# Filler matmuls and a re-weighted planner in a fused attention, MLP and convolution kernel

## The chip, the cores and the metric

One core of a Trainium2 chip runs the kernel. The metric is the device time of one execution in microseconds, median of three runs.

## The reference

Three stages follow one another, for 4 batches of 768 tokens and a model width of 384 (8 heads of 48):

```python
f = 1.0 / (1.0 + np.exp(-f_logit))                       # gated linear attention
for t in range(S):
    state = f[:, :, t, :, None] * state + np.einsum('bhd,bhe->bhde', k[:, :, t], v[:, :, t])
    y[:, :, t] = np.einsum('bhd,bhde->bhe', q[:, :, t], state)
...
xn = (x - mu) / np.sqrt(var + 1e-06) * g_ln              # layer norm, MLP of width 1536
x = x + np.maximum(xn @ w_ch1, 0.0) @ w_ch2
...
h = np.maximum(x @ w_in, 0.0)                            # width 1024
conv_out[s] = sum of conv_w[k] * h[s + k - 1], k = 0, 1, 2
out = (h * (1 / (1 + np.exp(-conv_out)))) @ w_out
```

The weights arrive as float64 and are decoded on the chip.

## The kernel before

The 3072 tokens are cut into 24 chunks of 128 (six to a batch), and three chunks make a unit, eight in all. `chunk(t)` (L467) computes the attention of one chunk: ScalarE (ACT) forms the gates, VectorE (DVE) runs two scans over them (L499, L501), GpSimd (POOL) or VectorE multiplies queries and keys by the products (L505, L507), two more VectorE operations finish the keys (L509, L511), and TensorE (PE) computes the scores (L525), the products of keys and values (L557 or L598 to L600) and the outputs (L626, L636 or L655). GpSimd computes the reciprocal deviation of the layer norm (L673, L677), and a transposing DMA brings the normalized chunk to the MLP.

`first(u)` is the first matrix of the MLP (L716 to L718, three half-precision products for one accurate one), `second(u, tt)` the second (L785 to L791), `gate(u)` the input matrix of the convolution (L845 to L847), the taps on VectorE (L862, L867), the gate, and the output matrix (L896 to L898). `prep1` and `prep` decode the weights in 22 pieces: a DMA brings a piece (L391), three VectorE operations decode it (L397, L400, L403), ScalarE and VectorE split it in a high and a low half, and for the first matrix TensorE forms the low half with diagonal matrices (L430, L431) that `diags` makes on ScalarE (L920). The conv table (L927 to L931) is one more small piece. The gates can't start before the last piece is decoded, since their buffers lie in the memory of the decoding.

No instruction order is written by hand. Every step is a `Job` with an engine, a guessed duration, a key, what it depends on and the buffers it takes. `Plan.run` (L172) simulates the engines with the guessed durations, and at every step issues the job that could start first; among jobs of one engine that could start within 0.1 us of the first, the one with the lowest key. The order so found is the program of each engine, and the hardware runs it with semaphores. The keys are due times in microseconds: `CP` and `CPL` are the pace of the chunks (`CPL` from the twelfth), `C1` and `C2` set the two MLP matrices of later units back, `H2` the gates, `O` the output matrix, `EV` brings evictions forward, `W1`, `W2` and `WI` are the due times of the weight pieces, whose loads have a key 30 lower. A job on POOL also sets the simulated VectorE back by a share of its duration. The six PSUM banks of pool `B` go to whatever asks first.

Of the kernel before, what the change touches and what calls it, by code (L numbers as in the profile page):

```python
# [9 lines left out]
F32 = mybir.dt.float32  # L10
F16 = mybir.dt.float16
BF16 = mybir.dt.bfloat16
# [7 lines left out]
B, H, S, D = 4, 8, 768, 48  # L20
DM = H * D
# [38 lines left out]
XN_ACT = range(0, 10)  # L60
X2_PE = range(0, 9)
OBX = 2
SW = CH + 1


CP = 22.6
CPL = 22.0
LATE = 12.0
T0 = 32.5
ATT = 0.3  # L70
C1 = 63.0
C2 = 19.7
H2 = -23.6
O = 46.1
EV = 38.7
W1 = 23.8
W2 = 52.3
WI = 95.7

def flat(a):  # L80
    return a.rearrange("p a b -> p (a b)")
# [2 lines left out]
def decode(nc, dst, tmp, raw):  # L84
    hi = raw[:, :, 1]
    nc.vector.tensor_scalar(
        out=tmp, in0=hi, scalar1=3, scalar2=0x3FFFFFFF,
        op0=ALU.logical_shift_left, op1=ALU.bitwise_and,
    )
    nc.vector.scalar_tensor_tensor(  # L90
        out=tmp, in0=hi, scalar=-0x40000000, in1=tmp, op0=ALU.bitwise_and, op1=ALU.bitwise_or
    )
    nc.vector.scalar_tensor_tensor(
        out=dst.bitcast(U32), in0=raw.bitcast(U32)[:, :, 0], scalar=29, in1=tmp.bitcast(U32),
        op0=ALU.logical_shift_right, op1=ALU.bitwise_or,
    )
# [19 lines left out]
class Job:  # L116
    def __init__(self, eng, dur, key, fn, deps, takes, uses, lat):
        self.eng, self.dur, self.key, self.fn, self.lat = eng, dur, key, fn, lat
        self.takes, self.uses = takes, uses
        self.left, self.then, self.ready, self.at = 0, [], 0.0, None  # L120
        for d in deps:
            d.then.append(self)
            self.left += 1


class Plan:
# [9 lines left out]
    def __init__(self):  # L136
        self.pools = {}
        self.n = 0
        self.jobs = []

    def slots(self, name, tiles):
# [20 lines left out]

    def start(self, j, free):
        t = max(j.ready, free)
        for p, k in j.takes:
            s = self.pools[p]
            if not s.free or (p not in self.ANY and s.order[0] != k):
                return None
            t = max(t, s.free[0][0])
        return t  # L170

    def run(self):  # L172
        ready = {e: [] for e in self.ENGINES}
        free = dict.fromkeys(self.ENGINES, 0.0)
        for j in self.jobs:
            if not j.left:
                ready[j.eng].append(j)
        todo = len(self.jobs)
        while todo:
            best = None  # L180
            for e in self.ENGINES:
                c = [(t, j.key, z) for z, j in enumerate(ready[e])
                     if (t := self.start(j, free[e])) is not None]
                if not c:
                    continue
                first = min(c)[0]
                pick = min((k, t, z) for t, k, z in c if t <= first + 0.1)
                if best is None or pick[1] < best[0]:
                    best = (pick[1], e, pick[2])
            assert best  # L190
            t, e, z = best
            j = ready[e].pop(z)
            for p, k in j.takes:
                s = self.pools[p]
                s.order.remove(k)
                s.held[k] = s.free.pop(0)[1]
            j.fn()
            j.at = t
            free[e] = t + j.dur
            if e == "POOL":  # L200
                free["DVE"] += 0.2 * max(0.0, j.dur - 0.8)
            end = t + j.dur + j.lat
            for p, k in (*j.takes, *j.uses):
                s = self.pools[p]
                s.users[k] -= 1
                s.last[k] = max(s.last.get(k, 0.0), end)
                if not s.users[k]:
                    s.free.append((s.last[k], s.held[k]))
                    s.free.sort()
            for x in j.then:  # L210
                x.left -= 1
                x.ready = max(x.ready, end)
                if not x.left:
                    ready[x.eng].append(x)
            todo -= 1
        return max(free.values())
# [3 lines left out]
def fast_path(  # L220
    ctx: ExitStack, tc: tile.TileContext, v, qk_, f_, gln, w1, w2, wi, cw, wo, out, bad
):
    nc = tc.nc
    const = ctx.enter_context(tc.tile_pool(name="const", bufs=1))
# [3 lines left out]
    P = Plan()  # L228
# [6 lines left out]
    V = lambda n: 0.07 + n * 1.04e-3  # L235
    V2 = lambda n: 0.07 + n * 0.53e-3
    A = lambda n: 0.1 + n * 0.833e-3
    G = lambda n: 0.15 + n * 2.2e-3

    fbs = bufs("fb", 2, [128, NP, SW], F32)  # L240
    qks = bufs("qk", 2, [128, 2, NP, CH], F32)
    nc.vector.memset(fbs[0][:, :, 0:1], 20.0)
    nc.vector.memset(qks[0], 0.0)
    mhalf = const.tile([128, 1], F32, name="mhalf")
    warm = const.tile([128, 1], F32, name="warm")
    nc.gpsimd.memset(mhalf, -0.5)
# [25 lines left out]
    gl8 = const.tile([128, KC], F32, name="gl8")  # L272
    cws = const.tile([128, M2, 3], F32, name="cws")
# [5 lines left out]
    pall = const.tile([128, NT, NP, 1], F32, name="pall")  # L279
# [37 lines left out]
    diag = pp.tile([128, KC, 128], F32, name="diag")  # L317
# [32 lines left out]
    J = {}  # L350
# [20 lines left out]
    def check_raw(g):  # L371
        nc.scalar.activation(  # L372
            out=g, in_=g, func=AF.Square, scale=RAW_MAX ** -0.5, accum_out=acc_col()
        )
        nc.scalar.activation(
            out=g, in_=g, func=AF.Exp, scale=-RAW_MAX / RAW_MIN, accum_out=acc_col()
        )

    def transfer(dur, key, fn, buf, size):
        j = P.job("SP", dur, key, fn, (), [buf], lat=1.0)  # L380
        return P.job("DMA", size / 2.8e5, key, lambda: None, [j], (), [buf], lat=1.2)

    def words(name, a, src, key):
# [83 lines left out]
    def chunk(t):  # L467
        b, c = divmod(t, NCH)
# [3 lines left out]
        key = due_att(t)  # L472
        N = NP * CH
        fb = lambda: flat(P("fb", t))
        e = lambda: flat(P("e", t))
# [5 lines left out]
        pend = lambda: P("e", t)[:, :, CH:]  # L481
# [6 lines left out]
        def tt(n, dk, fn, deps, takes=(), uses=(), pool=True):  # L488

            if pool:  # L490
# [8 lines left out]
        s1 = P.job("DVE", 1.14, key + 4, lambda: nc.vector.tensor_tensor_scan(  # L499
            e(), e(), flat(d1), 1.0, ALU.mult, ALU.max), [a2], (), [E_])  # L500
        s2 = P.job("DVE", 1.14, key + 5, lambda: nc.vector.tensor_tensor_scan(  # L501
            w(), w(), flat(d2), 1.0, ALU.mult, ALU.min), [a4], (), [W_])
        P.job("POOL", 0.8, key + 30, lambda: nc.gpsimd.tensor_copy(pall[:, t], pend()), [s1], (),
              [E_])
        qe = tt(N, 6, lambda v_: v_.tensor_tensor(out=q_(), in0=q_(), in1=e3(), op=ALU.mult),  # L505
                [s1, J["qk", t]], (), [E_, Q_], t in POOL_Q)
# [38 lines left out]
        if not last and not dma:  # L545
# [23 lines left out]
            else:  # L569
                j = dv(DM, 14, lambda: nc.vector.scalar_tensor_tensor(  # L570
                    out=tm()[:112], in0=kv3(), scalar=SY, in1=so()[:112], op0=ALU.mult,
                    op1=ALU.add), [kv, *old], (), [K_, KV, *SO])
# [88 lines left out]
        x = lambda: P("x", t)  # L661
# [3 lines left out]
        ST, RS = ("st", t), ("rs", t)  # L665
# [10 lines left out]
            )  # L676
            nc.gpsimd.tensor_tensor(out=rs, in0=rs, in1=mhalf, op=ALU.pow)  # L677
        bn = P.job("DVE", 0.69, key + 19, stats, [xc], [ST], [X_])
        rs = P.job("POOL", 1.0, key + 20, rstd, [bn], [RS], [ST])
        N_, XS = ("xn", t), ("xs", t)  # L680
        if t in XN_ACT:
            MB = ("mb", t)
            mb = P.job("POOL", 0.41, key + 20, lambda: nc.gpsimd.tensor_scalar(
                out=P(*MB), in0=mv[:, 0:1], scalar1=P(*RS), scalar2=-1.0, op0=ALU.mult,
                op1=ALU.mult), [rs], [MB], [RS])
            scaled = lambda o, dk, deps, takes, uses: act(
                DM, key + dk, o, x, AF.Identity, deps, takes, [*uses, X_, RS, MB],
                scale=lambda: P(*RS), bias=lambda: P(*MB))
            xn = scaled(lambda: P(*N_), 21, [mb], [N_], [])
            xh = scaled(lambda: P(*XS)[:, 0], 22, [mb], [XS], [])  # L690
            xh = P.job(None, 0.0, key + 22, lambda: None, [xn, xh])
        else:
            xn = dv(DM, 21, lambda: nc.vector.tensor_scalar(
                out=P(*N_), in0=x(), scalar1=mv[:, 0:1], scalar2=P(*RS), op0=ALU.subtract,
                op1=ALU.mult), [rs], [N_], [X_, RS], lambda n: 0.39)
            xh = act(DM, key + 22, lambda: P(*XS)[:, 0], lambda: P(*N_), AF.Copy, [xn], [XS], [N_])
# [218 lines left out]
    craw = const.tile([128, M2 * 3, 2], I32, name="craw")  # L915
# [4 lines left out]
    def diags():  # L920
# [2 lines left out]
                out=diag[:, kc, :], in_=ident, func=AF.Copy, scale=gl8[:, kc:kc + 1]  # L923
            )
        nc.scalar.activation(out=nident, in_=ident, func=AF.Copy, scale=-1.0)
    J["diag"] = P.job("ACT", 1.2, -10.0, diags, [J["gl8"]])
    cj = P.job("SP", 0.45, 20.0, lambda: nc.sync.dma_start(  # L927
        out=craw.rearrange("p n t -> p (n t)"), in_=cw.bitcast(I32)))
    cj = P.job("DVE", 0.5, 60.0, lambda: decode(nc, cws.rearrange("p a b -> p (a b)"), ctw, craw), [cj])

    P.job("ACT", 0.9, 70.0, lambda: check_raw(craw.bitcast(F32)[:, :, 1]), [cj])  # L931

    for m in range(6):
        J["w1", m] = prep1(m, W1 + 4.0 * m)
# [39 lines left out]
    for i, w_ in enumerate((w1s, w2s, wis, wos)):  # L974
        h_ = w_[:, 0].rearrange("p a b -> p (a b)")
        n = h_.shape[1] // 6
        for z in range(6):
            norm2(lambda h_=h_, z=z, n=n: h_[:, z * n:(z + 1) * n], n, 1.0, nrm[:, i, z:z + 1],
                  500.0 + z, [J["late"]])
    with tc.manual_schedule():  # L980
        P.run()

# [269 lines left out]
```

## Time and profile before

| | us |
|---|---|
| runs | 624.65, 625.05, 627.04 |
| median | 625.05 |
| profiled execution | 625.46 |
| its span | 623.8 |
| TensorE busy | 586.1 (94%) |
| VectorE busy | 495.9 (80%) |
| ScalarE busy | 395.7 (63%) |
| GpSimd busy | 95.4 (15%) |

The span runs from the first to the last instruction; the profiled execution's own time is 1.66 us longer. Busy shares are means over a front, in which VectorE is nearly always busy and TensorE has gaps, and a long later stretch in which TensorE has none. In the groups below, a time in square brackets at the end of a timeline row is how long the engine sat idle before it, and after the arrow stands what ended that.

### The profile page before, as it was taken

How to read it: one execution, taken by the hardware profiler on the slowest of the kernel's cores; microseconds unless marked ns; L12 is line 12 of the kernel's file. 1: busy time of each engine (PE TensorE's matmuls, PEld its weight loads, DVE VectorE, ACT ScalarE, POOL GpSimd, SP SyncE). 2: the span in 40 equal slices, each digit the busy share in tenths (PEclk: the TensorE clock that was granted, in tenths of full speed). 3: DMA queues.
4: the chain of work that ended last, by engine and by line, in shares of the span. 5: the costliest groups of instructions: out<-in, count | busy, mean ns of one | idle time of the engine just before them, and what ended most of it. 6: DMA issues, size and time to landing. Idle time of an engine off the chain costs nothing.

```text
span 623.8 us, 11788 instructions
## 1 busy us (share of the span) xinstructions
PE 586.1 (94%) x4698; PEld 398.0 (64%) x4698; DVE 495.9 (80%) x753; ACT 395.7 (63%) x808; POOL 95.4 (15%) x142
## 2 busy tenths in 40 slices
PE   0889999899899999999999999999999999999994
PEld 0769777677576666666666666666666666666562
DVE  4797999999998998599899995698996942315962
ACT  3697877789899975364596863554684722315762
POOL 4451342423343100100000100010000000000000
PEclk9998999899999999999999999999999999999999
DMA  8573746870234023453422106432311002002011
GB/s 222 162 184 119 230 147 168 232 193 14 56 84 115 22 59 100 102 104 89 94 56 68 56 14 124 110 78 59 68 40 56 14 1 64 25 1 40 1 38 44
DMA packets 77951, 53.83 MB, mean 86 GB/s; under 512 B 51520, under 2 KB 69952, under 8 KB 77888
## 3 DMA queue, kind: packets, MB, share of 16 engines
q1 hardware_dynamic: 77888, 53.00, 34.2%
q8 instruction: 39, 0.64, 0.4%
q14 instruction: 24, 0.20, 0.1%
HBM read 36.20 MB, written 4.72 MB: 66 GB/s over the span
## 4 chain that ended last, share of the span: by engine, by line
PE 69%; DVE 21%; ACT 3%; DMA 2%; issue 2%; POOL 1%; SPq 0%; POOLq 0%
PE B L716 6%; PE B L717 6%; PE B L718 6%; PE B L788 6%; PE B L790 6%; PE B L791 6%; PE B L845 4%; PE B L847 4%; PE B L846 4%; PE B L898 4%; PE B L896 4%; PE B L897 4%; PE sc__148 L525 3%; DVE tw L400 2%; PE B L626 2%
## 5 line engine op out<-in xcount | busy, mean ns | idle before, releaser
L716 PE MATMUL B<-xnT,w1s 128*128 128x128 f16 (+1 forms) x432 | 109.1, 275 | 1.3 <-DVE kts L570 1.3
L718 PE MATMUL B<-xnT,w1s 128*128 128x128 f16 (+1 forms) x432 | 109.1, 275 | 0.0
L717 PE MATMUL B<-xnT,w1s 128*128 128x128 f16 (+1 forms) x432 | 109.0, 274 | 0.0
L788 PE MATMUL B<-w2s,hh 128*128 128x384 f16 x288 | 94.2, 327 | 0.0
L790 PE MATMUL B<-w2s,hh 128*128 128x384 f16 x288 | 94.0, 326 | 0.0
L791 PE MATMUL B<-w2s,hh 128*128 128x384 f16 x288 | 93.9, 326 | 0.0
L896 PE MATMUL B<-wos,g 128*128 128x384 f16 x192 | 62.6, 326 | 1.1 <-ACT g L336 1.1
L898 PE MATMUL B<-wos,g 128*128 128x384 f16 x192 | 62.6, 326 | 0.5 <-DVE vr L1009 0.5
L845 PE MATMUL B<-x2T,wis 128*128 128x385 f16 x192 | 62.9, 328 | 0.0
L847 PE MATMUL B<-x2T,wis 128*128 128x385 f16 x192 | 62.9, 327 | 0.0
L846 PE MATMUL B<-x2T,wis 128*128 128x385 f16 x192 | 62.9, 327 | 0.0
L336 ACT ACTIVATE hh<-B 128x384 f16<-128x384 f32 (+1 forms) x90 | 44.8, 504 | 28.3 <-PE B L718 27.7
L897 PE MATMUL B<-wos,g 128*128 128x384 f16 x192 | 62.6, 326 | 0.0
L722 DVE SCALAR_TENSOR_TENSOR hh<-B,hh 128x384 f16<-128x384 f32 (+1 forms) x90 | 51.0, 576 | 14.3 <-ACT hh L336 14.1
L525 PE MATMUL sc__148<-qk 64*128 64x128 f32 x384 | 31.4, 308 | 24.5 <-DVE qk L511 15.9
L717 PEld LDWEIGHTS <-w1s 128*128 128x128 f16 x432 | 42.7, 99 | 14.9 <-issue 1.5
L716 PEld LDWEIGHTS <-w1s 128*128 128x128 f16 x432 | 43.1, 100 | 14.2 <-issue 0.2
L718 PEld LDWEIGHTS <-w1s 128*128 128x128 f16 x432 | 42.7, 99 | 14.0
L673 POOL TENSOR_SCALAR rs<-mvs 128x1 f32<-128x1 f32 x24 | 10.7, 444 | 243.3 <-DVE mvs L669 243.3
L525 PEld LDWEIGHTS sc__148<-qk 64*128 64x128 f32 x384 | 26.6, 209 | 31.1 <-issue 24.4
L862 DVE SCALAR_TENSOR_TENSOR cv<-hr,cws,cv 128x383 f32<-128x383 f32 (+1 forms) x56 | 35.8, 638 | 13.1 <-ACT cv L336 12.9
L788 PEld LDWEIGHTS <-hh 128*128 128x128 f16 x288 | 28.5, 99 | 18.7 <-ACT raw L372 0.3
(182 smaller groups left out, 1307.1 us busy)
## 6 DMA issues: line engine op xcount, KB each, us to landing
qk<-in_qk__dram SPq DMA_DIRECT2D x48, 192.0 KB, 3.6
raw<-in_w_dram SPq DMA_DIRECT2D x12, 768.0 KB, 5.1
fb<-in_f__dram SPq DMA_DIRECT2D x24, 256.0 KB, 3.3
vv<-in_v_dram SPq DMA_DIRECT2D x24, 192.0 KB, 2.6
out_dram<-ob SPq DMA_DIRECT2D x18, 192.0 KB, 2.0
raw<-in_wi_dram SPq DMA_DIRECT2D x6, 512.0 KB, 3.8
raw<-in_wo_dram SPq DMA_DIRECT2D x4, 768.0 KB, 4.7
out_dram<-x SPq DMA_DIRECT2D x6, 192.0 KB, 2.0
```

The costliest lines, as they stand in the source:

```text
L716: nc.tensor.matmul(o, w1s[:, 0, kc, ms], x0, start=(kc == 0), stop=False)
L717: nc.tensor.matmul(o, w1s[:, 0, kc, ms], x1, start=False, stop=False)
L718: nc.tensor.matmul(o, w1s[:, 1, kc, ms], x0, start=False, stop=(kc == KC - 1))
L788: nc.tensor.matmul(o(), h[:, 0], w2s[:, 0, m, :], start=(m == 0 and not pe), stop=False)
L790: nc.tensor.matmul(o(), h[:, 0], w2s[:, 1, m, :], start=False, stop=False)
L791: nc.tensor.matmul(o(), h[:, 1], w2s[:, 0, m, :], start=False, stop=(m == M1 - 1))
L845: nc.tensor.matmul(o, wis[:, 0, kc, ms], r0, start=(kc == 0), stop=False)
L846: nc.tensor.matmul(o, wis[:, 0, kc, ms], r1, start=False, stop=False)
L847: nc.tensor.matmul(o, wis[:, 1, kc, ms], r0, start=False, stop=(kc == KC - 1))
L896: nc.tensor.matmul(p, g[:, 0, ts_], wos[:, 0, m, :], start=(m == 0), stop=False)
L897: nc.tensor.matmul(p, g[:, 0, ts_], wos[:, 1, m, :], start=False, stop=False)
L898: nc.tensor.matmul(p, g[:, 1, ts_], wos[:, 0, m, :], start=False, stop=(m == M2 - 1))
```

## The change

Before a matmul job that the planner sees more than 1 us after the end of the one before, it now issues matmuls of a constant zero tile (128 by 128 against 128 by 384, bfloat16) into a PSUM bank that is free; nothing reads their results. Their number is the simulated gap times 0.75 (0.5 for the gap before the first job) divided by 0.165 us. The diagonals get the key 4.5 in place of -10, the conv table's load, decoding and check get keys 60, 100 and 110 in place of 20, 60 and 70. The planner's model is altered: engines start at given times and not at zero, a DMA issue waits for one of eight landing slots, a POOL job sets VectorE back by more, several POOL and VectorE durations are changed. All the due times have other values.

```diff
+DRAG = 0.35
-CPL = 22.0
+CPL = 18.3
-T0 = 32.5
-C1 = 63.0
-C2 = 19.7
-H2 = -23.6
-O = 46.1
-EV = 38.7
-W1 = 23.8
-W2 = 52.3
-WI = 95.7
+T0 = 32.4
+C1 = 70.0
+C2 = 24.8
+H2 = -9.5
+O = 81.1
+EV = 47.0
+W1 = 21.8
+W2 = 58.9
+WI = 93.7
...
+        self.land, self.count = dur + lat, 1
...
         t = max(j.ready, free)
+        if j.eng == "SP":
+            t = max(t, self.landed[j.count - 1])
...
         free = dict.fromkeys(self.ENGINES, 0.0)
+        free.update(SP=0.8, ACT=2.3, DVE=2.5, POOL=4.5)
+        self.landed = [0.0] * 8
...
+            if e == "PE" and t - free[e] > 1.0 and self.fill:
+                n = int((t - free[e]) * (0.75 if free[e] else 0.5) / 0.165)
+                x = self.pools["B"].free
+                if x and x[0][0] < free[e] - 0.5 or not free[e]:
+                    self.fill(n, self.pools["B"].tiles[x[0][1]])
+            if e == "SP":
+                self.landed = self.landed[j.count:] + [t + j.land] * j.count
...
             if e == "POOL":
-                free["DVE"] += 0.2 * max(0.0, j.dur - 0.8)
+                free["DVE"] += DRAG * max(0.0, j.dur - 0.8)
...
-    G = lambda n: 0.15 + n * 2.2e-3
+    G = lambda n: 0.15 + n * 2.75e-3
...
+    wm = const.tile([128, DM], BF16, name="wm")
+    nc.vector.memset(wm, 0.0)
...
+        j.land, j.count = size / 2.8e5 + 2.2, 2 if dur > 0.8 else 1
...
-        P.job("POOL", 0.8, key + 30, lambda: nc.gpsimd.tensor_copy(pall[:, t], pend()), [s1], (),
+        P.job("POOL", 0.5, key + 30, lambda: nc.gpsimd.tensor_copy(pall[:, t], pend()), [s1], (),
...
-        rs = P.job("POOL", 1.0, key + 20, rstd, [bn], [RS], [ST])
+        rs = P.job("POOL", 1.3, key + 20, rstd, [bn], [RS], [ST])
...
-            mb = P.job("POOL", 0.41, key + 20, lambda: nc.gpsimd.tensor_scalar(
+            mb = P.job("POOL", 0.6, key + 20, lambda: nc.gpsimd.tensor_scalar(
...
-    J["diag"] = P.job("ACT", 1.2, -10.0, diags, [J["gl8"]])
-    cj = P.job("SP", 0.45, 20.0, lambda: nc.sync.dma_start(
+    J["diag"] = P.job("ACT", 1.2, 4.5, diags, [J["gl8"]])
+    cj = P.job("SP", 0.45, 60.0, lambda: nc.sync.dma_start(
         out=craw.rearrange("p n t -> p (n t)"), in_=cw.bitcast(I32)))
-    cj = P.job("DVE", 0.5, 60.0, lambda: decode(nc, cws.rearrange("p a b -> p (a b)"), ctw, craw), [cj])
-    P.job("ACT", 0.9, 70.0, lambda: check_raw(craw.bitcast(F32)[:, :, 1]), [cj])
+    cj = P.job("DVE", 0.6, 100.0, lambda: decode(nc, cws.rearrange("p a b -> p (a b)"), ctw, craw), [cj])
+    P.job("ACT", 0.56, 110.0, lambda: check_raw(craw.bitcast(F32)[:, :, 1]), [cj])
...
+    def fill(n, bank):
+        for _ in range(n):
+            nc.tensor.matmul(bank[:, :DM], wm[:, :128], wm, start=True, stop=True)
+    P.fill = fill
```

## Rows read from the trace of the kernel before

**Rows 1.** Stretches: length; busy PE, PEld, DVE, ACT, POOL; granted clock; DMA share; GB/s.
```profile
0.00:16.00 16.00, 0.11 (x2) 0.14 (x2) 7.82 (x11) 6.30 (x14) 7.33 (x33) 1.00 0.83 226
...
15.89:32.36 16.47, 15.16 (x73) 12.46 (x74) 12.93 (x18) 10.68 (x24) 7.19 (x7) 1.00 0.50 147
...
46.01:52.84 6.83, 6.00 (x46) 5.44 (x47) 4.54 (x7) 4.30 (x9) 0.00 (x0) 0.50 0.67 211
...
114.28:117.69 3.41, 3.41 (x20) 2.22 (x19) 3.38 (x7) 3.38 (x9) 1.28 (x3) 0.50 0.94 294
...
16.00:48.00 32.00, 27.55 (x196) 23.43 (x198) 26.16 (x36) 25.60 (x58) 14.63 (x14) 0.97 0.65 170
48.00:192.00 144.00, 134.89 (x1355) 105.00 (x1351) 138.53 (x188) 120.38 (x260) 47.85 (x47) 0.97 0.49 137
192.00:610.00 418.00, 417.74 (x3117) 266.45 (x3118) 321.06 (x514) 241.15 (x477) 25.61 (x49) 1.00 0.26 58
```

**Rows 2.** Timeline of all engines up to the first scores: start, duration, engine, line, operation.
```profile
1.12 0.91 DVE L243 MEMSET qk<- 128x1024 f32 x1 [0.18 <-issue]
4.48 0.62 SPq L391 DMA_DIRECT2D raw<-in_w_dram  x1
6.85 0.98 ACT L922 ACTIVATE diag<-ident,gl 128x128 f32<-128x128 f32 x3 [1.40 <-DVE gl L917]
7.94 0.62 ACT L336 ACTIVATE e<-e 128x516 f32<-128x516 f32 x1
8.66 1.23 DVE L499 TENSOR_TENSOR_SCAN e<-e,d 128x516 f32<-128x516 f32 x1 [1.91 <-ACT e L336]
9.91 2.60 SPq L927 DMA_DIRECT2D craw<-in_cw_dram  x1
11.05 1.48 DVE L507 TENSOR_TENSOR qk<-qk,w 128x512 f32<-128x512 f32 x1
13.16 0.56 DVE L397 TENSOR_SCALAR tw<-raw 128x768 int32<-128x768 int32 x1 [0.62 <-DMA raw<-in_w_dram]
15.11 0.68 DVE L511 SCALAR_TENSOR_TENSOR qk<-w,qk 128x512 f32<-128x512 f32 x1
```

**Rows 3.** Timeline of PE, at places where it comes out of a gap, and one without.
```profile
15.89 2.08 PE L525 MATMUL sc__148<-qk 64*128 64x128 f32 x16 [15.89 <-DVE qk L511]
...
46.84 2.08 PE L525 MATMUL sc__148<-qk 64*128 64x128 f32 x16 [3.14 <-issue]
...
114.02 1.88 PE L525 MATMUL sc__148<-qk 64*128 64x128 f32 x16 [2.04 <-issue]
...
131.41 1.16 PE L525 MATMUL sc__148<-qk 64*128 64x128 f32 x16 [0.81 <-POOL mb L683]
...
170.52 1.03 PE L557 MATMUL B<-vv,kts 128*112 128x96 f32 x8 [2.65 <-ACT kts L336]
```

**Rows 4.** Timeline of PE, single matmuls of 384 columns around 117.69 us.
```profile
117.26 0.53 PE L788 MATMUL B<-w2s,hh 128*128 128x384 f16 x1
117.58 0.38 PE L790 MATMUL B<-w2s,hh 128*128 128x384 f16 x1
...
117.97 0.33 PE L788 MATMUL B<-w2s,hh 128*128 128x384 f16 x1
118.13 0.33 PE L790 MATMUL B<-w2s,hh 128*128 128x384 f16 x1
```

**Rows 5.** Timeline of all engines, POOL and DVE ahead of 46.84 us.
```profile
40.29 1.49 POOL L507 TENSOR_TENSOR qk<-qk,w 128x512 f32<-128x512 f32 x1
...
43.27 1.41 DVE L509 TENSOR_TENSOR w<-w,e 128x512 f32<-128x512 f32 x1
...
46.06 0.68 DVE L511 SCALAR_TENSOR_TENSOR qk<-w,qk 128x512 f32<-128x512 f32 x1
```

**Rows 6.** Timeline of all engines at the end.
```profile
611.75 0.34 PE L896 MATMUL B<-wos,g 128*128 128x384 f16 x1 [1.12 <-ACT g L336]
...
612.74 0.34 PE L898 MATMUL B<-wos,g 128*128 128x384 f16 x1 [0.49 <-DVE vr L1009]
...
617.50 0.49 ACT L336 ACTIVATE x<-B 128x384 f32<-128x384 f32 x1 [1.46 <-PE B L898]
```

More of the change, by code (lines that the diff above doesn't have):

```diff
@@ L138, in __init__ @@
         self.n = 0
+        self.fill = None
         self.jobs = []
```

## The prediction, made before the result was known

> **What bounds the kernel now.** I read the stretches first, then TensorE's waits, the timeline of the start, and that of the end. The stretches [rows 1] split the execution in two. From 192 to 610 us TensorE is busy 417.74 of 418.00 us at the granted clock 1.00: nothing but TensorE's own work counts there. Before 192 us it loses time in two ways. It is idle: 15.89 us before its first matmul [rows 3], 32.00 - 27.55 = 4.45 us from 16 to 48 and 144.00 - 134.89 = 9.11 us from 48 to 192 us. And it runs at the lower clock level (1.2 GHz) in three stretches. Two read 0.50 in the clock column; in the one from 15.89 to 32.36 us the column reads 1.00, but the sixteen score matmuls at 15.89 take 2.08 us, as those at 46.84 under 0.50 do, against 1.16 at 131.41 [rows 3]. Half of the busy time in these three is what the full clock would give back at most: 15.16/2 = 7.6, 6.00/2 = 3.0 and 3.41/2 = 1.7 us [rows 1].
>
> So a gain must come from before 192 us or from the end. There it has a second limit: VectorE is busy 138.53 of 144 us from 48 to 192 us and 26.16 of 32 from 16 to 48 [rows 1]. It must do attention, decoding and splitting before TensorE has a stock of work, so TensorE can be made ready earlier by what VectorE waits and no more: 5.84 us before 48, 5.47 after, besides the start.
>
> The sum is made against the profiled execution, 625.46 us (span 623.8 and 1.66 around it); it lies 0.41 above the median of 625.05.
>
> **Start: diagonals and load order (-1.2 us).** ScalarE finishes the two gate activations, waits 1.40 us for the scaled layer-norm weights, makes the diagonals from 6.85 on, and only then, at 7.94, the activation that the first scan (8.66) waits for [rows 2]. With key 4.5 the diagonals come behind chunk 0's activations (keys 1 to 4). The wait of 1.40 and the diagonals' 7.94 - 6.85 = 1.09 us go, so the scan starts near 6.2 and the key product, now 11.05 to 12.53, ends near 10.1. But the next VectorE instruction is the decoding of the first weight piece, which waits for its DMA until 13.16 [rows 2]; the scores come 15.89 - 13.16 = 2.73 us behind it. Its place need not change: key products and the step after them are still 0.13 us apart in the planner, more than its 0.1 us window. Its load is now due at 21.8 - 30 = -8.2, ahead of the load of chunk 1's gates (-7.7): it is issued some 0.6 us earlier with 262 KB less before it, 1.16 us at 226 GB/s [rows 1]. I take landing near 12.0, and first scores at 12.0 + 2.73 = 14.7. Bounds: 0 if the landing stays, -4.5 if the decoding goes behind the keys (10.1 plus two 0.6 us steps is 11.4). Chunk 1's gates land up to 3.5 us later (786 KB at that rate); ScalarE reads them right after chunk 0's, but nothing on VectorE uses them before 16.58, so this is hidden unless the start comes in at its lower bound.
>
> The other moves of this kind I cost at nothing. The conv table's issue leaves SP's queue at 9.91 (2.60 us) [rows 2]; all loads of chunks 0 and 1 and of three weight pieces stand before it, so nothing that I count on comes earlier. Its three small VectorE operations move into a stretch as full as the one they leave, and its DMA, decoding and check are not used before the first gate.
>
> **The filler (-2.3 us at the start, +0.5 for its price).** It waits only for a VectorE memset behind the one that ends at 2.03 [rows 2], in time that VectorE now idles, so it starts near 2.3 us. A 384-column matmul takes 117.58 - 117.26 = 0.32 us at half clock and 118.13 - 117.97 = 0.16 at the full one [rows 4]. The count is half the simulated gap at 0.165 each: a gap of 12 to 15 us gives 36 to 45 matmuls. All of them at half clock would last 11.5 to 14.4 us and end, counted from 2.3, between 13.8 and 16.7; if the clock rises after some 5 us, near 11. So there may be 0 to 4 us idle between filler and scores, or, at worst, 2 us in which the scores stand behind it in TensorE's queue and VectorE's mask, the first user of the scores, behind them.
>
> Whether the clock stays up decides. After 3.14 us of idle it came back low, after 2.04 us too, but after 2.65 us not: 1.03 us for eight key-value matmuls at 170.52 [rows 3]; length alone doesn't tell. The Trainium skill ("TensorE: Matmul & The Clock Gate", section "HAM oscillation — how this bites in real kernels") says that a kernel whose matmul bursts stand between waits for DMA is throttled again in every wait, which speaks against a burst that ends before a DMA wait. The trace agrees at 46.84 and differs at 170.52; by the rule alone this term is 0. Bounds 0 and -7.6; I take -2.3, near the lower, since the first stretch is made of chains through ScalarE and VectorE in which a faster matmul shortens only its own link.
>
> Later fillers occur where the planner foresees more than 1 us. Each takes three quarters of the simulated gap at full clock, one and a half times it at half clock. Where the gap is not real, they are pure loss: a fancied gap of 3 us costs 2.25. I put 0.5 us, bounds 0 and 4.
>
> **The gap at 43.7 us (-3.5 us).** The longest wait after the start is 3.14 us, and the half-clock stretch behind it costs up to 3.0 more [rows 1, 3]. The scores at 46.84 waited for the keys finished at 46.74; that VectorE step stands behind a POOL key product of 1.49 us and a VectorE product that took 1.41 us while POOL ran, against 0.68 for the step after it [rows 5]. The planner priced that POOL product at 0.15 + 512 x 0.0022 = 1.28 and now at 1.56; so it should order around it or fill the gap. Bounds 0 and -6.1. With the start's 2.3 I take 3.5, together 5.8, the whole of VectorE's idle time from 16 to 48 us.
>
> **The new order from 48 to 192 us (-1 us).** Other due times move decoding, attention and eviction against each other. I cannot follow each job; the same work stays, TensorE has 9.11 us idle plus 1.7 of half clock here, VectorE 5.47 us. Bounds: -5.5 (VectorE never waits) and +6 (another two thirds of today's idle). I take -1.
>
> **From 192 us, and the end (-1.6 us).** In the saturated stretch an order costs nothing so long as something is ready. At the end the last output products wait 1.12 and 0.49 us for the last gate's low half [rows 6]. Now unit 6's output products have key h2 + 81.1, which lies beyond the keys of unit 7's gate matmuls (67.8 behind unit 6's, to 81.8): about 72 products of 0.16 us, 11.7 us, remain for TensorE during the last gate chain, and the 1.61 us go. What follows the last matmul (its copy at 617.50 and the way out) stays. Bounds -1.6 and +3, should the later gates lengthen the last chain.
>
> **Sum.** -1.2 - 2.3 + 0.5 - 3.5 - 1 - 1.6 = -9.1; 625.46 - 9.1 = 616.4 us.
>
> **Rivals.** *The front gives little* (0.22): the clock falls back before the first scores, and only part of the 43.7 us gap closes: -1.2 - 1.5 - 1.6 + 0.5 = -3.8, 621.7 us. For it: VectorE's 96% from 48 to 192 us, and the DMA wait at 13.16; against it: TensorE's two losses there are large. That the filler does nothing at all, because no gap over 1 us is simulated besides the first, is in this case.
>
> *The front is cleared* (0.18): the decoding moves behind the first keys (-4.5), all of VectorE's waits from 16 to 192 us go (-11.3), and the end gains 1.6: -17.4, 608.1 us. For it: the planner now knows when loads land and what POOL costs; against it: VectorE never ran below 4% idle for so long a stretch.
>
> *Starvation in the middle* (0.15), the other sign: gates and output products are due later (by 14.1 and 49.1 us), and attention of the later chunks earlier (18.3 in place of 22.0 us a chunk). VectorE, now 77% busy from 192 to 610 us, gets its attention work bunched, with less output work on TensorE to cover it. Where TensorE idles at the 48 to 192 us rate, 9.11/144 = 6.3%, it loses 6.3 us per 100 us; with the forecast's gain of 9.1 the kernel is slower once this lasts over 145 us. Over 210 us (192 to 400) it costs 13.2: 629.6 us. Against it: TensorE's idle time there is 0.26 us now, so there is stock.
>
> **Chances and range.** The forecast has 0.45. A difference of 0.5%, 3.1 us, is what a measurement of this kernel can tell from none, so faster is below 621.9 and slower above 628.2. Faster: 0.43 of the forecast, half of the first rival, all of the second: 0.72. Within: the rest of these and a quarter of the last: 0.16. Slower: 0.12. The range 606 to 628 leaves out the far half of the starvation case and the tips of the others.
>
> **What would show it.** Right: first scores at 14 to 15 us with ScalarE's diagonals behind them; scores of about 1.2 and not 2.08 us at the first or second chunk; no 0.50 stretch after 40 us; TensorE without idle time from 192 us or earlier; no wait before the last output products. Wrong: first scores at 2 us per sixteen and a decoding still waiting at 13; filler directly followed by a matmul that was long ready; TensorE gaps after 192 us; VectorE below 90% from 48 to 192 us with TensorE waiting on it.

## The result and the profile after

The changed kernel takes 616.98 us (median of 4 runs, 616.05 to 620.65) against 624.85 us of the kernel before on the same chip (4 runs, 624.30 to 627.04): ratio 0.9876, 95% interval 0.9852 to 0.9899, which is clear of noise. The profiled execution has 616.58 us, 8.88 less than that of before, at a span of 614.7 us.

The stretches of the kernel after, with the columns of [rows 1]. The second and third line are cut where the trace's record of the granted clock changes: it begins with a rise at 8.24 us, falls at 15.06 and rises at 25.30. Ahead of its first entry the column reads 1.00 even where matmuls run at half speed, as in [rows 1]. The last line runs past the last matmul, which ends at 607.33 us.

```profile
0.00:16.00 16.00, 10.92 (x56) 6.08 (x57) 9.66 (x13) 7.87 (x17) 7.33 (x33) 0.97 0.88 233
8.24:15.06 6.82, 4.04 (x34) 2.58 (x33) 5.99 (x8) 2.08 (x5) 2.88 (x15) 1.00 1.07 266
15.06:25.30 10.24, 9.55 (x43) 7.84 (x40) 7.89 (x12) 5.27 (x11) 4.26 (x5) 0.50 0.90 257
16.00:48.00 32.00, 29.55 (x239) 24.30 (x238) 27.62 (x41) 26.69 (x61) 12.84 (x13) 0.85 0.66 188
48.00:192.00 144.00, 135.60 (x1378) 104.74 (x1375) 140.27 (x192) 124.37 (x266) 51.19 (x51) 1.00 0.50 136
192.00:610.00 418.00, 415.28 (x3088) 263.83 (x3088) 317.37 (x511) 237.96 (x467) 26.42 (x45) 1.00 0.26 59
```

One stretch at half clock is left, 15.06 to 25.30 us; the stretches at 46.01 and 114.28 of [rows 1] have no successor. TensorE's idle time from 16 to 48 us fell from 4.45 to 32.00 - 29.55 = 2.45 us, though 3.58 us of that busy time are filler, and from 48 to 192 us from 9.11 to 8.40. VectorE is still 97% busy there (140.27 of 144).

The timeline of all engines at the start, to be held against [rows 2]:

```profile
2.02 0.22 DVE L259 MEMSET wm<- 128x192 uint32 x1
5.53 0.62 ACT L352 ACTIVATE e<-e 128x516 f32<-128x516 f32 x1
6.77 1.23 DVE L516 TENSOR_TENSOR_SCAN e<-e,d 128x516 f32<-128x516 f32 x1
6.95 0.99 ACT L939 ACTIVATE diag<-ident,gl 128x128 f32<-128x128 f32 x3 [0.28 <-DVE gl L934]
9.16 1.49 DVE L524 TENSOR_TENSOR qk<-qk,w 128x512 f32<-128x512 f32 x1
11.44 0.56 DVE L414 TENSOR_SCALAR tw<-raw 128x768 int32<-128x768 int32 x1 [0.79 <-DMA raw<-in_w_dram]
13.39 0.69 DVE L528 SCALAR_TENSOR_TENSOR qk<-w,qk 128x512 f32<-128x512 f32 x1
```

The diagonals now stand behind the activation that the scan needs. The scan starts 1.89 us earlier (not at 6.2 us as forecast, since VectorE first does a small step that waits for the layer-norm weights until 6.69) and the key product ends at 10.65 in place of 12.53. The decoding of the first weight piece still waits 0.79 us for its DMA, which lands 1.72 us earlier, and the scores start 2.74 us behind it, as before.

TensorE's timeline, to be held against [rows 3]:

```profile
2.30 9.09 PE L1000 MATMUL B<-wm 128*128 128x384 bf16 x37 [2.30 <-DVE wm L259]
14.18 1.30 PE L542 MATMUL sc__150<-qk 64*128 64x128 f32 x16 [2.79 <-issue]
...
17.21 1.81 PE L574 MATMUL B<-vv,kts 128*112 128x96 f32 x8 [0.69 <-ACT kts L352]
18.81 3.54 PE L653 MATMUL B<-vv,am 128*128 128x48 f32 x16
...
25.40 2.44 PE L1000 MATMUL B<-wm 128*128 128x384 bf16 x14
...
30.98 1.14 PE L1000 MATMUL B<-wm 128*128 128x384 bf16 x6
...
46.54 1.16 PE L542 MATMUL sc__150<-qk 64*128 64x128 f32 x16 [1.73 <-issue]
```

The first burst, 37 matmuls, raises the clock at 8.24 us but ends at 11.39; TensorE idles 2.79 us, the clock falls inside the first scores, and the products after them run at half speed. Two later bursts, 14 and 6 matmuls, are all that the planner adds.

The end, all engines, to be held against [rows 6]:

```profile
603.86 4.23 SPq L925 DMA_DIRECT2D out_dram<-x  x3
607.13 0.19 PE L1029 MATMUL sc__150<-vst,one 128*1 128x6 f32 x2
607.24 0.49 ACT L352 ACTIVATE x<-B 128x384 f32<-128x384 f32 x1 [1.46 <-PE B L915]
607.99 0.14 DVE L1034 TENSOR_SCALAR bad<-vr 1x1 int32<-1x1 f32 x1
```

The output products end without a wait. Behind them now stands the verdict: a matmul and five small VectorE steps, of which the last ends at 608.13, 6.5 us before the span's end.

**Where the time went.** TensorE's last instruction ends at 607.33 in place of 617.47, 10.14 us earlier. The lines add up to this: its first real matmul comes 1.71 us earlier; it idles 10.90 in place of 15.44 us after that (-4.54), the 1.61 us of [rows 6] included; it is busy 9.55 us at half clock in place of 15.16 + 6.00 + 3.41 = 24.57 [rows 1], half of the difference is -7.51; and the two later bursts add 2.44 + 1.14 = 3.58. Together -10.18. From the last matmul to the end of the span it takes 7.33 in place of 6.29 us, +1.05, so the span shrinks by 9.1. The two profiles are one execution each: that of before has a granted clock of 0.991, while most other runs of that kernel have 0.981 to 0.989.

### The profile page after: what moved, and what is told of

Its sections match the earlier page's. It is cut to its first block, busy times and chain, and to the rows that moved or that the text cites. A ratio compares the mean times of both kernels' runs of the same rounds, so it can differ in the third digit from the quotient of the medians.

```text
span 614.7 us, 11928 instructions
## 1 busy us (share of the span) xinstructions
PE 591.3 (96%) x4755; PEld 398.9 (65%) x4755; DVE 494.9 (81%) x754; ACT 396.9 (65%) x808; POOL 97.8 (16%) x142
## 4 chain that ended last, share of the span: by engine, by line
PE 73%; DVE 17%; ACT 3%; issue 3%; POOL 1%; DMA 1%; SPq 0%; DVEq 0%; POOLq 0%
PE B L733 6%; PE B L805 6%; PE B L735 6%; PE B L734 6%; PE B L808 6%; PE B L807 6%; PE B L913 5%; PE B L915 5%; PE B L914 5%; PE B L862 4%; PE B L863 4%; PE B L864 4%; PE sc__150 L542 3%; DVE tw L417 2%; PE B L1000 2%
## 5 line engine op out<-in xcount | busy, mean ns | idle before, releaser
L733 PE MATMUL B<-xnT,w1s 128*128 128x128 f16 (+1 forms) x432 | 108.0, 273 | 3.7 <-DMA xnT<-xs 3.7
L735 PE MATMUL B<-xnT,w1s 128*128 128x128 f16 (+1 forms) x432 | 107.9, 273 | 0.0
L734 PE MATMUL B<-xnT,w1s 128*128 128x128 f16 (+1 forms) x432 | 107.9, 273 | 0.0
L690 POOL TENSOR_SCALAR rs<-mvs 128x1 f32<-128x1 f32 x24 | 13.4, 557 | 198.3 <-DVE mvs L686 198.2
L805 PEld LDWEIGHTS <-hh 128*128 128x128 f16 x288 | 28.4, 99 | 18.7
L808 PEld LDWEIGHTS <-hh 128*128 128x128 f16 x288 | 28.2, 98 | 18.6
L807 PEld LDWEIGHTS <-hh 128*128 128x128 f16 x288 | 28.2, 98 | 18.5 <-issue 2.0
L352 ACT ACTIVATE hr<-B 128x385 f32<-128x385 f32 x52 | 25.2, 484 | 15.9 <-PE B L864 14.5
```

The costliest lines, as they stand in the source:

```text
L733: nc.tensor.matmul(o, w1s[:, 0, kc, ms], x0, start=(kc == 0), stop=False)
L734: nc.tensor.matmul(o, w1s[:, 0, kc, ms], x1, start=False, stop=False)
L735: nc.tensor.matmul(o, w1s[:, 1, kc, ms], x0, start=False, stop=(kc == KC - 1))
L805: nc.tensor.matmul(o(), h[:, 0], w2s[:, 0, m, :], start=(m == 0 and not pe), stop=False)
L807: nc.tensor.matmul(o(), h[:, 0], w2s[:, 1, m, :], start=False, stop=False)
L808: nc.tensor.matmul(o(), h[:, 1], w2s[:, 0, m, :], start=False, stop=(m == M1 - 1))
```

## The experiments

In each group of runs the kernel before ran beside them, at medians of 625.49 to 625.85 us. Ratios are to it; the changed kernel has 0.9876 [0.9852, 0.9899]. Since that was measured in a group of its own, beside 624.85 us, differences between kernels are given by the ratios too (0.001 is 0.63 us). The profile of a kernel is one execution of it.

**1. No filler.**

```diff
-    P.fill = fill
```

> The changed kernel with its 57 filler matmuls left out; plan and order of all other instructions stay. Theory A (the filler gives back clock at the start): the first scores stay at 14.2 us, but the half clock lasts past 25.3 us, to about 32 as before the change, and the time rises by 2 to 5 us, to 619 to 622. Theory B (the gain is the new order alone): within 1 us of 617.

Measured 622.07 us (618.15 to 626.08), ratio 0.9944 [0.9923, 0.9966]. TensorE's timeline, then three stretches with the columns of [rows 1], all of this kernel. The first ends where its clock record begins, with a rise:

```profile
14.21 2.08 PE L542 MATMUL sc__150<-qk 64*128 64x128 f32 x16 [14.21 <-DMA raw<-in_w_dram]
```

```profile
14.21:26.63 12.42, 11.73 (x54) 10.00 (x55) 9.26 (x14) 6.14 (x14) 4.35 (x6) 1.00 0.72 225
98.31:101.72 3.41, 3.41 (x33) 3.40 (x32) 3.38 (x6) 1.92 (x6) 1.54 (x1) 0.50 0.72 149
135.85:139.27 3.42, 2.72 (x26) 2.72 (x26) 3.42 (x5) 3.15 (x7) 0.46 (x1) 0.50 0.48 121
```

The scores start where they do in the changed kernel, at half clock, and two later stretches fall to 0.50. The filler is worth 4.3 us by the ratios, whose intervals lie apart, and 5.1 by the medians; the order without it about 3.5. There is no stretch at 0.50 near 46 us in this profile either.

Where the filler's gain arises is not shown. At the start half clock lasts until 26.63 us, not to about 32 as expected, so the bursts save (11.73 - 9.55)/2 = 1.1 us there. The two later stretches would make (3.41 + 2.72)/2 = 3.1 us more, but experiment 8, which has the bursts, shows both of them too. And three runs of experiment 1 with a granted clock of 0.995 to 0.997, which leaves no room for both (half of their 6.83 us is 0.55% of the span), took 620.11, 620.41 and 622.27 us, against 620.61 of the profiled run.

**2. A first burst that reaches the scores.**

```diff
-                n = int((t - free[e]) * (0.75 if free[e] else 0.5) / 0.165)
+                n = int((t - free[e]) * (0.75 if free[e] else 0.71) / 0.165)
```

> The changed kernel with the first burst 52 matmuls long in place of 37 (factor 0.71 for 0.5), so that it ends near 13.8 us and not at 11.4, just ahead of the first scores. Theory A: the clock does not fall at 15.1 us, chunk 0's TensorE work takes half as long, the chain through it shortens by 2 to 4 us, 613 to 615. Theory B (VectorE bounds the front, TensorE's clock in it doesn't matter): 617 within 1 us. A burst that delays the first scores by more than 0.5 us would show in the scores' start.

Measured 614.49 us (612.75 to 620.67), ratio 0.9849 [0.9812, 0.9886]. TensorE's timeline, and one stretch from the clock's rise on:

```profile
2.30 11.35 PE L1000 MATMUL B<-wm 128*128 128x384 bf16 x52 [2.30 <-DVE wm L259]
14.25 1.16 PE L542 MATMUL sc__150<-qk 64*128 64x128 f32 x16 [0.61 <-issue]
...
16.69 1.02 PE L574 MATMUL B<-vv,kts 128*112 128x96 f32 x8 [0.69 <-ACT kts L352]
17.55 1.91 PE L653 MATMUL B<-vv,am 128*128 128x48 f32 x16
...
25.52 1.16 PE L542 MATMUL sc__150<-qk 64*128 64x128 f32 x16 [0.46 <-POOL mb L700]
```

```profile
7.87:600.00 592.13, 579.77 (x4732) 392.13 (x4730) 491.40 (x745) 391.45 (x797) 92.42 (x124) 1.00 0.36 87
```

With 52 matmuls 0.61 us of idle time is left, the clock doesn't fall before the end, and the second chunk's scores come at 25.52 in place of 29.39 us. The profiled run is the pure case (612.99 us at a granted clock of 0.998); the other five have 0.982 to 0.993 and reach 620.67. Against the changed kernel this gains 2.5 us by the medians and 1.7 by the ratios, with intervals that overlap. It shows what the changed kernel's burst leaves, not that every run gets it.

**3. The filler alone, in the old order, with the old planner model.**

> The kernel before with the filler alone (the old planner's gaps give bursts of 37, 14, 6 and 9). Theory A: the first burst ends near 11.4 us, 4.5 us ahead of the first scores at 15.9, the clock falls back, and only the second burst of 14 raises it; 622 to 624.5. Theory B: 625 within 1 us, or above it by the bursts' own time, up to 2 us.

Its edit adds to the kernel before only what the filler needs:

```diff
...
+    wm = const.tile([128, DM], BF16, name="wm")
+    nc.vector.memset(wm, 0.0)
...
+    P.fill = fill
```

Measured 624.87 us (622.51 to 627.07), ratio 0.9995 [0.9979, 1.0011]: nothing. TensorE's timeline:

```profile
15.28 2.08 PE L533 MATMUL sc__150<-qk 64*128 64x128 f32 x16 [3.92 <-issue]
...
44.74 1.22 PE L533 MATMUL sc__150<-qk 64*128 64x128 f32 x16 [3.53 <-issue]
```

In its profile the burst ends at 11.35 with the scores at 15.28, 3.92 us later; the clock falls at 14.99, rises at 18.4 and falls again at 45.7 and 110.6, near where it falls in [rows 1]. That profile (622.87 us, granted clock 0.990) is one of the kernel's two fastest runs; nine of the twelve have 0.974 to 0.983. So the same rule for the bursts buys nothing in the old order and 4 to 5 us in the new one. That the new order gains by keeping TensorE supplied after the bursts is a reading, not tested by itself.

**4 and 5. The due times without the model, and the model without the due times.** The first is the changed kernel with the ten old constants, the second the kernel before with the ten new ones (and the diagonals and the conv table where the old kernel has them). `CP` is 22.6 in both kernels; the other ten due times are those that changed.

```diff
-CPL = 18.3
+CPL = 22.0
...
-O = 81.1
+O = 46.1
...
```

> The changed kernel (new planner model, filler, diagonals and conv table later) with the ten old due times. If the due times carry the gain after the start: 621 to 626, with TensorE waits from 48 to 192 us as before (about 9 us) and the wait ahead of the last output products back (1.6 us). If the model carries it: 617 to 619.

> The kernel before with the ten new due times alone (old planner model, no filler, diagonals and conv table early). It closes the square with the kernel before (old, old), the run with the old due times in the new model (628.3) and the changed kernel without its filler (new, new: 622.1). If the due times are good by themselves: 620 to 623. If they fit only the model they were found with: 625 or above.

Measured 628.28 us for the new model with old times (626.71 to 630.37), ratio 1.0042 [1.0023, 1.0060], and 631.19 for the old model with new times (629.37 to 633.33), ratio 1.0091 [1.0073, 1.0110]. Both are slower than the kernel before: the first lies above both of its ranges, the second is as expected of times that fit only their model. The timeline of the former:

```profile
20.94 0.18 DVE L87 TENSOR_SCALAR ctw<-craw 128x24 int32<-128x24 int32 x1 [6.02 <-DMA craw<-in_cw_dram]
...
22.74 0.66 PE L653 MATMUL B<-vv,am 128*128 128x48 f32 x2 [2.97 <-DVE am L547]
```

and stretches of either, first new model with old times, then old model with new times, with a line of the latter's timeline:

```profile
16.00:48.00 32.00, 28.34 (x203) 22.74 (x200) 25.15 (x35) 22.27 (x53) 9.34 (x11) 0.78 0.55 154
```

```profile
48.00:192.00 144.00, 129.34 (x1323) 100.24 (x1321) 136.17 (x187) 120.27 (x260) 46.77 (x49) 0.99 0.50 132
```

```profile
214.44 1.11 PE L550 MATMUL B<-ident,qk 128*128 128x128 f32 x4 [3.65 <-DVE hh L722]
```

In the former VectorE, working in program order, waits 6.02 us for the conv table's DMA, TensorE 2.97 behind it, at half clock; the planner also sees more gaps and issues 87 filler matmuls in place of 57. In the latter TensorE idles 144.00 - 129.34 = 14.66 us between 48 and 192 us, against 9.11, and once more for 3.65 us at 214.44. Neither half is a gain by itself: 625.5 with both old, 628.3 (with filler) and 631.2 (without) mixed, 617.0 with both new (622.1 without filler). The square isn't pure, since only one of the mixed kernels has filler, and what each of the waits costs wasn't tested.

**6. The diagonals where they were.**

```diff
-    J["diag"] = P.job("ACT", 1.2, 4.5, diags, [J["gl8"]])
+    J["diag"] = P.job("ACT", 1.2, -10.0, diags, [J["gl8"]])
```

> The changed kernel with the diagonals' key back at -10. Forecast's theory (the first weight piece's landing sets the first scores, so the diagonals' 1.1 us on ScalarE are hidden up to that): key product ends near 12.5 instead of 10.6, after the landing at 11.4, so the first scores come about 1 us later, 15 to 15.5, and the time is 617.5 to 619. Rival (the diagonals were the whole start): first scores at 15.9 or later and 619 or more.

Measured 619.48 us (619.32 to 620.21), ratio 0.9907 [0.9892, 0.9921]. Its timelines of VectorE and TensorE:

```profile
12.62 0.55 DVE L414 TENSOR_SCALAR tw<-raw 128x768 int32<-128x768 int32 x1
...
15.34 2.08 PE L542 MATMUL sc__150<-qk 64*128 64x128 f32 x16 [3.98 <-issue]
```

The decoding now stands behind the late key product without a wait for its DMA, and scores come 15.34 - 12.62 = 2.72 us after it. The edit costs 2.5 us by the medians and 1.9 by the ratios, with intervals that just touch; the time is above the forecast theory's range, the scores are within it. That this is more than the 1.16 us by which the scores are later may come from the idle time behind the burst, which grows to 3.98 us; it wasn't tested.

**7. The long burst, and the verdict ahead of the last twelve output matmuls.** To experiment 2 is added, where the last unit's output products are issued:

```diff
...
+                    if tt == UT - 1 and u == NU - 1 and m0:
+                        P.verdict()
...
```

> The changed kernel with the first burst of 52 and with the verdict (the reductions over the check values, one matmul and five small VectorE operations) issued ahead of the last twelve output matmuls and not behind them. If the verdict ends last in the changed kernel: the time from the last output matmul to the end of the span falls from 7.3 to about 6.3 us and the time is about 1 us below that of the long burst alone (614.5), 613 to 614. If the last output transfer ends last: no difference, 614 to 615.

Measured 612.32 us (610.05 to 617.89), ratio 0.9795 [0.9761, 0.9828], the lowest median here and clear of the changed kernel's interval. The end of it, all engines:

```profile
606.27 0.19 PE L1026 MATMUL sc__150<-vst,one 128*1 128x6 f32 x2
...
607.20 0.14 DVE L1031 TENSOR_SCALAR bad<-vr 1x1 int32<-1x1 f32 x1
...
608.55 0.49 ACT L352 ACTIVATE x<-B 128x384 f32<-128x384 f32 x1 [1.69 <-PE B L917]
```

The last matmul ends at 608.52 and the span at 614.61: 6.09 us in place of 7.33, and of 7.05 in experiment 2. The verdict's 1 us is confirmed. The profiled run (616.32 us) is one whose first weight piece was decoded late:

```profile
12.72 0.56 DVE L414 TENSOR_SCALAR tw<-raw 128x768 int32<-128x768 int32 x1 [2.12 <-DMA raw<-in_w_dram]
...
15.45 1.99 PE L542 MATMUL sc__150<-qk 64*128 64x128 f32 x16 [3.05 <-issue]
```

Its clock falls at 15.58 us and, behind a wait of 2.71 us, again at 46.30: the stretch near 46 us can come back in the new order.

**8. A control: one constant moved by 0.1.**

```diff
-T0 = 32.4
+T0 = 32.5
```

> Control for the planner: the changed kernel with T0 = 32.5 in place of 32.4, a difference without meaning of its own. If the plan is insensitive: within 1 us of 617. If any small change of a key reshuffles the order, it lies 2 us or more off, and differences of that size between plans say nothing of a single key.

Measured 617.59 us (615.27 to 621.81), ratio 0.9876 [0.9848, 0.9903], and the same three bursts. In the two traces the instructions of every engine come in the same order, so this is the changed kernel measured again: its time is confirmed, and what another order behind a small change of a key would cost isn't tested. It shows instead how far two executions of one order differ. Its clock falls at 13.14 us and in two later stretches, of which the profile of the changed kernel has none. These are its stretches and TensorE's timeline:

```profile
98.47:101.88 3.41, 3.41 (x36) 3.41 (x34) 3.38 (x6) 2.07 (x7) 1.54 (x1) 0.50 0.67 192
136.02:139.43 3.41, 3.07 (x29) 3.07 (x28) 3.41 (x4) 3.14 (x6) 0.03 (x1) 0.50 0.38 100
```

```profile
136.36 0.27 PE L733 MATMUL B<-xnT,w1s 128*128 128x128 f16 x1 [2.90 <-DMA xnT<-xs]
```

and the same place in the changed kernel, where the clock stayed at 1.00:

```profile
135.68 0.22 PE L733 MATMUL B<-xnT,w1s 128*128 128x128 f16 x1 [3.05 <-DMA xnT<-xs]
```

**9. Keys ahead of the decoding.** The first two decoding steps are issued behind chunk 0's keys.

```diff
...
+        if t == 0:
+            first_ = kn.fn
+            kn.fn = lambda: [z() for z in (first_, *held)]
```

> The changed kernel with one swap in VectorE's program and nothing else: the first two operations of the first weight piece's decoding come behind chunk 0's keys, not between them. Forecast's theory of the start (the decoding's wait for its DMA holds the first scores): scores at 11.9 us in place of 14.2, right behind the burst that ends at 11.4, so the clock is still up at chunk 0; VectorE itself gains only the 0.8 us that it waited. Time 613 to 615.5. Rival: TensorE now waits longer behind the scores, the clock falls there, 616 to 617.5. If the scores don't move, the theory of the start is wrong.

Measured 616.05 us (614.93 to 618.12), ratio 0.9852 [0.9828, 0.9876]. Timeline of TensorE:

```profile
12.48 1.16 PE L554 MATMUL sc__150<-qk 64*128 64x128 f32 x16 [1.70 <-issue]
...
16.31 1.81 PE L586 MATMUL B<-vv,kts 128*112 128x96 f32 x8 [1.81 <-ACT kts L352]
```

The scores come 1.70 us earlier, as meant. The time lies in the rival's range: TensorE waits 1.81 us behind the scores, and the clock falls at 13.81 and stays at 0.50 until 24.05. Against the changed kernel this gains 0.9 us by the medians and 1.5 by the ratios, and the intervals overlap.

**10. Only the first burst.**

```diff
-            if e == "PE" and t - free[e] > 1.0 and self.fill:
+            if e == "PE" and not free[e] and self.fill:
```

> The changed kernel with the first burst of 37 alone, without the 14 and 6 later fillers. The first burst alone lets the clock fall before the first scores. If the later fillers give back the clock in the first chunks: near the kernel with no filler, 620 to 622. If the first burst does it: 616 to 618.

Measured 618.40 us (616.02 to 620.17), ratio 0.9880 [0.9856, 0.9904]. The later bursts are worth 1.4 us by the medians and 0.3 by the ratios, with intervals that overlap; neither a gain nor a price of theirs is shown. The first burst alone makes 3.7 us by the medians and 4.0 by the ratios, clear of experiment 1. But its profile has the first scores at half clock as experiment 1 has, behind 3.52 us of idle time, and half clock until 26.21 us:

```profile
13.67 2.08 PE L542 MATMUL sc__150<-qk 64*128 64x128 f32 x16 [3.52 <-issue]
```

So that the first burst pays is shown, and how it pays is open.

**11 and 12. Keys first and the early verdict, with 37 and with 48 matmuls.** The order of experiment 9 with the verdict moved as in experiment 7; the second also with

```diff
-                n = int((t - free[e]) * (0.75 if free[e] else 0.5) / 0.165)
+                n = int((t - free[e]) * (0.75 if free[e] else 0.65) / 0.165)
```

> Chunk 0's keys ahead of the first decoding, and the verdict ahead of the last twelve output matmuls; first burst 37. If both act alone: 1 us below the kernel with the keys first, and about 6.1 us from the last output matmul to the end. Theory of the start: 612 to 614.5; rival: 615 to 616.5.

> Keys first, verdict early, and the first burst 48 long in place of 37, so that it reaches the earlier scores (12.1 to 12.5 us). If the clock fell in the keys-first kernels only because the burst ended 1.7 us too early: no fall before 16 us, chunk 0's TensorE work at full clock, 610.5 to 612.5. If the 1.3 to 1.8 us wait behind the scores is enough to let it fall: 613.5 to 614.5, as with the burst of 37.

Measured 614.29 us (612.27 to 617.86), ratio 0.9811 [0.9779, 0.9844], and 615.79 (612.16 to 617.36), ratio 0.9831 [0.9798, 0.9863]. The first is in the range of the theory of the start only by its median: three runs took 612.27 to 612.31 us at a granted clock of 0.993 to 0.996, three 616.27 to 617.86 at 0.982 to 0.985. The second, meant to be the best of all, gained nothing and lies above both of its ranges. Its timeline of TensorE, and the stretch after it:

```profile
12.36 1.16 PE L554 MATMUL sc__150<-qk 64*128 64x128 f32 x16
...
16.97 1.81 PE L586 MATMUL B<-vv,kts 128*112 128x96 f32 x8 [2.86 <-ACT kts L352]
```

```profile
16.96:27.20 10.24, 10.23 (x40) 8.06 (x41) 8.53 (x14) 5.52 (x12) 5.76 (x6) 0.50 0.67 177
```

The burst reaches the scores, but these now run ahead of the decoding, VectorE and ScalarE are late with what follows, and TensorE idles 2.86 us behind the scores: the hole has moved to the other side of them.

## Why the prediction was right, and where it was not

The time (616.4 forecast, 616.98 measured) and the mechanism of the start and of most of the end hold; the split of the gain does not, and how the filler pays is not what was forecast. That the sum is off by 0.6 us only is in part luck: the filler gave more than its term, and the end gave 1.05 us less.

*Start (-1.2).* Right: the landing sets the first scores (14.18 us, forecast 14.7), and the step behind it takes 2.74 us. Experiment 6 puts the diagonals' place at 1.9 to 2.5 us, of which 1.16 are the later scores. The lower bound, keys ahead of the decoding, exists too (experiment 9), and buys less than the time by which it moves the scores.

*Filler (-2.3 and +0.5).* The term failed in size. In the new order the bursts are worth 4.3 to 5.1 us net (experiment 1) in place of 1.8, between the bounds. The risk named, 0 to 4 us of idle time behind the burst, came true at 2.79 us, and the first scores' products still ran at half clock. The mechanism named, a faster clock at the start, accounts for 1.1 us of this in the profiles; the profile of experiment 8, with the bursts, has half clock from 13.14 to 26.79 us. Sparing later falls of the clock doesn't explain the rest, since experiment 8 has these too. The price is not measurable (experiment 10).

*Gap at 43.7 us (-3.5).* The half-clock stretch behind it went, the wait fell from 3.14 to 1.73 us: 1.4 and 3.0, so 4.4 by the rows. But the profile of experiment 1 has no such stretch without the filler, and that of experiment 3 has it with the filler in the old order; so it goes with the order, if not in every run (experiment 7 has it at 46.30). Whether the new price of the POOL product is what reordered this place wasn't tested by itself. The forecast tied both to one sum of 5.8. Filler, price and gap together were forecast at -5.3.

*48 to 192 us (-1).* 0.71 us of idle time and the 1.7 of half clock went in the profiled run; VectorE's waits shrank from 5.47 to 3.73 us, so the bound by VectorE holds. The half clock comes back in experiment 8, in other places, (3.41 + 3.07)/2 = 3.2 us of it, so this term isn't settled by one profile.

*The end (-1.6).* The two waits went as foreseen. The sentence that what follows the last matmul stays was wrong: the old kernel ended on its output copies, and once these came earlier, the verdict behind the last matmul ended last, 1.05 us dearer. Net 0.56 us; experiment 7 gets the rest back.

*Rivals.* Starvation fell: TensorE has no gap after 192.01 us. It does occur when the due times are taken without the model, mostly between 48 and 192 us and once behind that (experiment 5). Of the front that gives little one half came true, the clock that falls at the first scores; the other, a gap at 43.7 us that only partly closes, did too (1.73 us are left), but the half clock behind it went. The cleared front didn't come: VectorE still waits 3.73 us from 48 to 192, and its decoding ahead of the first keys, once moved (experiment 9), gains 0.9 to 1.5 us and not 4.5.

**Open.** Why one wait drops the clock and another does not; where in the execution the 4 to 5 us of the filler arise, given that the half-clock stretches of experiments 8 and 10, which have the first burst, are much like those of experiment 1; and what each due time, cost and key of the new order does by itself.

## What to carry to other kernels

A filler depends on the order around it: here it gave 4 to 5 us in the new order and nothing in the old one. Reaching the first real matmul with it (experiment 2) helped by the medians, not clear of noise, and didn't help where TensorE then waited behind that (experiment 12). Judge it by the clock column after the first real work, not by the clock at its own end, and by many runs, since one profile shows one course of the clock. Fit due times and the planner's costs together; each alone made this kernel slower. After removing a wait at the end, read again what ends last. Before calling a small change of a constant a control, check that it changes the order.

## What the runs showed of the hardware

Idle time of 1.70 us (experiment 9), 2.79 (the changed kernel) and 2.86 (experiment 12) was followed by a fall to 0.50; 3.05 us before the matmul at 135.68 us of the changed kernel was not, as its 1.00 from 48 to 192 us shows. At the same matmul of the same order, 2.90 us did drop the clock in experiment 8. The Trainium skill ("TensorE: Matmul & The Clock Gate", section "HAM oscillation — how this bites in real kernels") has matmul bursts between waits for DMA throttled again in every wait; of these last two waits, both for a DMA, the one in experiment 8 agrees and the one in the changed kernel differs.

Runs of experiment 7 spread with TensorE's mean granted clock: 610.05 us at 0.999, 612.86 at 0.994 and 617.89 at 0.990. The link is not strict: experiment 2 has 612.99 us at 0.998 and 612.75 at 0.993, and runs of the kernel before took 623.40 us at 0.984 and 627.31 at 0.988. In the profiled run of experiment 7 the first landing was about a microsecond late (decoding at 12.72 in place of 11.44 us), TensorE idled 3.05 us behind the burst, and the clock fell twice.
